# Fetching both x tiles ahead of the first K row, with dummy matmuls in between, in a linear-attention kernel

## The chip, the cores and the metric

The kernel runs on one core of a Trainium2 chip. The metric is the device time of one execution in microseconds (us), as the median of several. TensorE is called PE in the profile, VectorE DVE, ScalarE ACT, GpSimd POOL, and SyncE's DMA queue SPq. The "clock" of TensorE is the rate at which its matmuls follow one another; in these traces it has a slow and a fast value, 0.107 and 0.056 us for 128 columns.

## The reference, cut to what matters

```python
x = A_x                                             # 1 x 2048 x 1024
g = sigmoid((x * gate_w).sum(-1, keepdims=True))
a = linear_attention(x, wqkv) @ wo                  # 32 heads of 32
b = x + (gated MLP of the one row with the highest x @ w_r, put back)
return g * a + (1 - g) * b
```

Only the very start matters here: K and V are `x @ wqkv`, and this kernel feeds x to TensorE with its columns on the partitions. The sixteen x tiles have 128 rows each. Most are brought in transposed by DMA; the first two are loaded as they are and transposed on TensorE, so that work can begin early.

## The kernel before

The loads, all on SyncE's queue, 256 KB each (`load_k(c)` loads rows 128c to 128c+127 of the K weights):

```python
load_x(0, 1)
load_k(0)
load_x(1, 1)
for c in range(1, KC):          # KC = 8
    load_k(c)
# then a part of V's columns, the transposing loads, the rest of V, wq
```

TensorE's program, whose order is fixed:

```python
warm(N_WARM)                    # 6 dummy matmuls of 512 columns
...
def first_mm(t, c0, c1):        # tile t, K rows c0 to c1-1
    for c in range(c0, c1):
        for nb in range(2):
            kv_mm(first[t][nb], t, nb, c, c + 1)      # 128x512

unit_T(0)                       # 8 transposes of x tile 0, then two copies
warm(3, 128)                    # 3 dummies of 128 columns
first_mm(0, 0, 1)
wps = ps_ffn.tile([P, 16], BF, tag="f")
pe.transpose(wps[:], wrg_rows[:], ident[0:16, 0:16])
dve.tensor_copy(...)
unit_T(1)
for c in range(1, KC):
    first_mm(0, c, c + 1)
    if c < KC - 1:
        first_mm(1, c - 1, c)
es = [phi_exp(first[0][nb][:]) for nb in range(2)]
first_mm(1, 6, 8)
# ... from here on the V, K, Q and output blocks, not touched
```

I call the 32 matmuls of `first_mm` the first block: two tiles, eight K rows, two halves. In the profile's lines `warm_ps` marks the dummies, `xnat` an x tile as loaded, `pst` its transposes, `wps` the small transpose, `wkv` the K and V weights, `first` the first block and `ps` the blocks after it. `x8` means eight instructions merged into one line.

## Time and profile before

| | before |
|---|---|
| median of 3 runs (range) | 249.49 us (248.97 to 249.51) |
| span of the profiled execution | 247.7 us |
| TensorE busy | 98% of the span |
| the first block enters its dense run at, ends at | 7.17 us, 13.81 us |
| K row 1 lands at | 7.13 us |

The lines behind these numbers are in the prediction. The end of the first block is read as the start of the piece that follows it in the chain of waits (13.81, `PE ps`).

### The profile page before, as it was taken

What the parts mean: (1) busy time and instruction counts of PE and PEld (TensorE: products, weight loads), DVE (VectorE), ACT (ScalarE), POOL (GpSimd) and SP (SyncE); (2) the same over time, 40 slices, a digit from 0 to 9 for tenths busy, and PEclk for the clock granted to TensorE, in tenths of its full rate; (3) what the DMA queues carried; (4) which work ended last, traced back from release to release, by engine and by line L of the source; (5) the groups of instructions that cost most, each with busy time, mean ns of one, the idle gap of its engine ahead of it and who ended that gap; (6) DMA issues with size and microseconds to landing.
All of it is one profiled execution on the core that took longest, in us unless ns stands there. A gap on an engine that the chain in (4) does not pass through costs nothing.

```text
span 247.7 us, 4893 instructions
## 1 busy us (share of the span) xinstructions
PE 242.3 (98%) x1923; PEld 123.6 (50%) x1923; DVE 172.7 (70%) x264; ACT 127.6 (52%) x215; POOL 52.6 (21%) x100
## 2 busy tenths in 40 slices
PE   7999999999999999999999999999999999999994
PEld 3465756754554554554554555544443444444442
DVE  0043125279985879845989999996779999954342
ACT  3095434456565466544565555668887633333300
POOL 6000000300000100000013300101666689950000
PEclk9999999999999999999999999999999999999999
DMA  6999994399969992589659892000004654564122
GB/s 193 352 229 201 260 393 157 101 337 335 275 178 314 343 288 76 155 294 396 227 166 425 298 252 58 3 2 24 0 3 127 196 181 155 150 192 168 47 83 86
DMA packets 46311, 47.78 MB, mean 193 GB/s; under 512 B 16776, under 2 KB 35472, under 8 KB 46224
## 3 DMA queue, kind: packets, MB, share of 16 engines
q1 hardware_dynamic: 45648, 46.28, 61.1%
q0 software_dynamic: 608, 1.19, 1.8%
q8 instruction: 15, 0.25, 0.4%
q14 instruction: 8, 0.07, 0.1%
q10 hardware_dynamic: 32, 0.00, 0.0%
HBM read 39.33 MB, written 8.39 MB: 193 GB/s over the span
## 4 chain that ended last, share of the span: by engine, by line
PE 95%; DMA 2%; SPq 1%; DVE 0%; issue 0%; DVEq 0%
PE ps L83 88%; PE first L83 3%; PE kvacc L83 2%; DMA wkv<-in_A_wqkv_dram 2%; PE red L83 1%; PE dps L83 1%; PE pm L83 1%; SPq L83 1%; DVE ot L83 0%; PE yps L83 0%; DVEq L737 0%; PE pt L83 0%; PE hps L83 0%; PE rps L83 0%; PE xs_ps L83 0%
## 5 line engine op out<-in xcount | busy, mean ns | idle before, releaser
L83 PE MATMUL ps<-wkv,xT 128*128 128x352 bf16 (+2 forms) x608 | 106.5, 334 | 0.0
L83 PEld LDWEIGHTS <-xT 128*128 128x128 bf16 x640 | 62.2, 98 | 49.3 <-issue 0.6
L83 ACT ACTIVATE u<-ps 128x512 f32<-128x512 f32 x60 | 35.9, 598 | 46.4 <-PE ps L83 46.2
L83 PE MATMUL ps<-xT,wq 128*128 128x512 bf16 x256 | 58.4, 379 | 0.0
L83 PE MATMUL ps<-m_sb,pq_all 128*128 128x512 bf16 (+2 forms) x264 | 55.6, 373 | 0.0
L83 ACT ACTIVATE e<-u 128x512 f32<-128x512 f32 x64 | 40.3, 630 | 2.0
L83 PEld LDWEIGHTS <-pq_all 128*128 128x128 bf16 x264 | 25.4, 98 | 30.2 <-issue 0.7
L640 POOL TENSOR_TENSOR pq_all<-pq_all,rb 128x512 bf16<-128x512 bf16 x32 | 36.5, 1166 | 12.1 <-DVE rb L83 11.7
L83 PEld LDWEIGHTS <-wq 128*128 128x128 bf16 x256 | 24.4, 98 | 28.4 <-issue 1.4
L83 DVE SCALAR_TENSOR_TENSOR gacc<-wt,hcol,gacc 128x1024 f32<-128x1024 bf16 x27 | 34.5, 1279 | 0.4
L83 DVE SCALAR_TENSOR_TENSOR ot<-ps,gate,xg 128x512 bf16<-128x512 f32 (+2 forms) x33 | 23.5, 723 | 14.3 <-PE ps L83 14.2
L83 DVE SCALAR_TENSOR_TENSOR gacc<-wt,xs_f,gacc 128x2048 f32<-128x2048 bf16 x14 | 32.8, 2346 | 0.2
L83 ACT ACTIVATE xg<-xt,omg 128x1024 f32<-128x1024 bf16 x16 | 18.1, 1146 | 26.9 <-DVE ot L83 25.9
L83 DVE SCALAR_TENSOR_TENSOR pq_all<-ps,e 128x512 bf16<-128x512 f32 x32 | 21.9, 686 | 11.3 <-ACT e L83 11.3
L83 DVE SCALAR_TENSOR_TENSOR pk<-ps,e 128x512 bf16<-128x512 f32 x28 | 19.1, 686 | 11.8 <-ACT e L83 11.8
L83 DVE STREAM_SHUFFLE rb<-rdp 128x512 f32<-128x512 f32 x32 | 22.5, 731 | 0.0
L83 ACT CAST vt<-ps 128x352 bf16<-128x352 f32 x32 | 14.4, 453 | 11.5 <-PE ps L83 11.1
L214 POOL MEMSET vt<- 128x22 bf16 x16 | 3.8, 441 | 75.8 <-PE kvacc L83 75.3
L83 ACT CAST vc<-ps 128x320 bf16<-128x320 f32 x16 | 6.5, 428 | 7.3 <-PE ps L83 7.3
L83 DVE COPY rg<-ps 128x2 f32<-128x2 f32 x16 | 2.5, 159 | 10.2 <-ACT vc L83 10.1
L355 POOL DMA_DIRECT2D xs<-in_A_x_dram x1 | 0.7, 711 | 39.8 <-DVE sig L83 39.8
L83 DVE SCALAR_TENSOR_TENSOR pk<-first,e 128x512 bf16<-128x512 f32 x4 | 2.8, 692 | 8.2 <-ACT e L83 8.2
(100 smaller groups left out, 94.0 us busy)
## 6 DMA issues: line engine op xcount, KB each, us to landing
wt<-in_B_w_down_dram SPq DMA_DIRECT2D x14, 512.0 KB, 5.5
wt<-in_B_w_gate_dram SPq DMA_DIRECT2D x8, 512.0 KB, 7.4
wt<-in_B_w_up_dram SPq DMA_DIRECT2D x8, 512.0 KB, 6.4
xt<-xp SPq DMA_DIRECT2D x16, 256.0 KB, 2.6
out_dram<-ot SPq DMA_DIRECT2D x15, 256.0 KB, 2.0
wt<-in_B_w_gate_dram SPq DMA_DIRECT2D x8, 384.0 KB, 7.8
wt<-in_B_w_up_dram SPq DMA_DIRECT2D x8, 384.0 KB, 7.1
wkv<-in_A_wqkv_dram SPq DMA_DIRECT2D x8, 256.0 KB, 5.1
```

The source lines that it names most:

```text
L83: inst = fn(*a, **k)
L214: nc.gpsimd.memset(vt_t[t][:, :, 32:33], 1.0)
L355: nc.gpsimd.dma_start(out=xs8[:], in_=x2d[bass.ds(idx_val, 1), :].rearrange("o (c p) -> (o c) p", p=P))
L640: nc.gpsimd.tensor_tensor(sl, sl, rb[:], op=ALU.mult)
```

## The change

The intent: have the transposes of x tile 1 done before the K rows come, and keep TensorE busy meanwhile, so that its clock rises early. The whole diff:

```diff
     load_x(0, 1)
-    load_k(0)
     load_x(1, 1)
-    for c in range(1, KC):
+    for c in range(KC):
         load_k(c)
@@
     unit_T(0)
-    warm(3, 128)
-    first_mm(0, 0, 1)
-    wps = ps_ffn.tile([P, 16], BF, tag="f")
+    wps = ps_t.tile([P, 16], BF, tag="t")
     pe.transpose(wps[:], wrg_rows[:], ident[0:16, 0:16])
     dve.tensor_copy(wkv[:, :, 2 * D : 2 * D + 2], wps[:].rearrange("p (w c) -> p c w", w=2))
+    warm(2, 128)
     unit_T(1)
+    warm(4, 128)
+    first_mm(0, 0, 1)
     for c in range(1, KC):
```

## The prediction

> **What bounds the kernel now.** I read four views in this order: the page's first two parts, the chain of the work that ended last, the timeline of the first microseconds, and the single transfers that this timeline waits for.
>
> The page says which engine fills the span.
>
> ```profile
> span 247.7 us, 4893 instructions
> PE 242.3 (98%) x1923; PEld 123.6 (50%) x1923; DVE 172.7 (70%) x264; ACT 127.6 (52%) x215; POOL 52.6 (21%) x100
> PE   7999999999999999999999999999999999999994
> ```
>
> TensorE (PE) is busy 98% of the time, and only the first and the last of the 40 slices have holes. The change touches nothing but the start, so the question is what ends the start. The chain of waits, cut to its head, answers it (start, length, what).
>
> ```profile
> 1.90 0.45 SPq L83
> 2.35 0.04 issue
> 2.40 4.73 DMA wkv<-in_A_wqkv_dram
> 7.13 0.04 issue
> 7.17 6.64 PE first L83 x30
> 13.81 22.67 PE ps L83 x152
> ```
>
> From 7.17 us on, the chain is nearly all TensorE to 243.6 us. Before that it is one transfer: the weight row issued at 2.40 us and landed at 2.40 + 4.73 = 7.13 us. That is the fourth load on SyncE's queue, K row 1 (the order is x tile 0, K row 0, x tile 1, K row 1). So nothing that TensorE does before 7.13 us sets the end, unless it is still doing it then. The timeline of TensorE shows what it does.
>
> ```profile
> 1.02 2.72 PE L83 MATMUL warm_ps<-const-bfloat16-1.0 128*128 128x512 bf16 x6 [1.02 <-PEq L726]
> 3.88 1.03 PE L83 MATMUL pst<-ident,xnat 128*128 128x128 bf16 x8
> 4.71 0.53 PE L83 MATMUL warm_ps<-const-bfloat16-1.0 128*128 128x128 bf16 x3
> 5.03 0.85 PE L83 MATMUL first<-wkv,xT 128*128 128x512 bf16 x2
> 5.81 0.18 PE L83 MATMUL wps<-ident,wrg_rows 16*128 16x16 bf16 x1
> 6.36 0.62 PE L83 MATMUL pst<-ident,xnat 128*128 128x128 bf16 x8 [0.37 <-DMA xnat<-in_A_x_dram]
> 7.17 6.64 PE L83 MATMUL first<-wkv,xT 128*128 128x512 bf16 x30 [0.19 <-DMA wkv<-in_A_wqkv_dram]
> ```
>
> The reader is to see two holes ended by a transfer: 0.37 us for x tile 1 before its eight transposes, and 0.19 us for K row 1 before the dense run. The transposes of tile 1 end at 6.98 us, only 0.19 us ahead of the start that K row 1 allows. After it, 30 matmuls take 6.64 us, or 0.22 us each, without a wait.
>
> The times from issue to landing, asked one transfer at a time, are 2.8 us for x tile 0 (landed near 3.8), 3.0 for K row 0 (1.45 + 3.0 = 4.45), 4.4 for x tile 1 (1.90 + 4.4 = 6.3), 4.7 for K row 1 and 5.0 for K row 2 (2.87 + 5.0 = 7.87). The third load is the odd one, 1.85 us behind the second, where the others come about 0.7 us apart.
>
> **What the Trainium skill says.** "DMA: Bandwidth & Descriptors", section "Why a DMA increments its semaphore by 16 and not by 1", says that a transfer is spread over up to 16 DMA engines that finish independently, and that only the full count means that all has landed. So a load is as late as its slowest engine. This trace agrees at least with landings that don't come evenly: the third load took 4.4 us against 3.0 for the second, at equal size (256 KB).
>
> The same page, section "Queues, rings and completion order", says that on each DMA engine the descriptors are consumed in ring order. Then the landing of the fourth load depends on the bytes ahead of it, not on which tensor they belong to: this is what my prediction rests on. In the trace the loads land in the order of issue; no run here yet shows what a swap does.
>
> "TensorE: Matmul & The Clock Gate", section "Part 1: The HAM clock gate (the "warmup" mystery)", says that TensorE runs at half its clock until it has been busy for a window of about 3.4 us that runs freely. The trace agrees in the durations: the two matmuls on K row 0 start 0.42 us apart (5.03 and 5.45), those after 7.17 us come 0.22 us apart, so the clock rose somewhere between 5.4 and 7.2 us. This is what the dummy matmuls are for.
>
> **The change, part by part.**
>
> The load order becomes x tile 0, x tile 1, K row 0, K row 1, and so on. All four are 256 KB on the same queue, issued at the same four moments. If a place in the queue keeps its landing time, x tile 1 lands at 4.45 us in place of 6.3, K row 0 at 6.3 in place of 4.45, and K row 1 stays at 7.13. Later loads wait for older transfers to return their semaphores, but these are counted by place too (I compared the two built programs), so the queue's later schedule stays.
>
> On TensorE the six first dummies stay. Working with the slow rate, 0.107 us for 128 columns (the three dummies from 4.71 to 5.03 us):
> - The transposes of tile 0 run as before, to 4.71 us.
> - The small transpose of the router's and gate's rows comes next, ahead of K row 0 in place of after it: some 0.08 us, to 4.8. Its two little loads are on the other queue, issued before 1.9 us. I take them as landed, as the trace shows no wait for them at 5.81 us but can't show when they came.
> - Two dummies, 2 x 0.107 = 0.21, to 5.0 us. x tile 1 has been there since 4.45, so no wait is left: the 0.37 us hole is gone.
> - Eight transposes of tile 1, 8 x 0.107 = 0.86, to about 5.86 us. Their copies on VectorE (0.42 us) and ScalarE (0.59 us) end by about 6.5. The buffers that they need were freed by copies that end near 5.1 us.
> - Four dummies: 0.22 us if the clock is up by then, 0.43 if not: to 6.1 or 6.3 us.
> - K row 0 lands at 6.3 us: two matmuls, 2 x 0.22 = 0.43, to about 6.75.
> - Then TensorE is idle to 7.17, because the next in its program order is the pair of tile 0 on K row 1. The pair of tile 1 on K row 0, which could fill this hole, stands after that pair in the program.
>
> Removed: a 0.37 us wait. Added: three dummies net, 3 x 0.107 = 0.32 us, and a new hole of about 0.4 us. All of it lies ahead of 7.13 us, beside the transfer that sets it. The number of real matmuls left at 7.17 us is 30 in both kernels: 30 x 0.22 = 6.64 us, to 13.81. So the sum on the path is 0.0 us. What it buys is room: TensorE is ready for K row 1 at 6.75 in place of 6.98 us, 0.42 in place of 0.19 us ahead. In an execution where x tile 1 comes late, or K row 1 early, this is worth up to 0.2 us; I allow 0.1 us for it.
>
> After 13.81 us the order of instructions on every engine is the same in both built programs.
>
> **The rivals.**
>
> First rival, the intent: with both x tiles transposed early, the K stream starts sooner. It would need K row 1 to land sooner, since the program order holds all else behind it. For it speaks the odd 1.85 us step before the third load: if the slow share belongs to reading x tile 1 and not to the place in the queue, K rows 0 and 1 could come up to about 0.4 us earlier. Against it, K row 1 came only 0.8 us after x tile 1, so the engines had moved on. It would give about 248.9 us.
>
> Second rival, the clock: if the holes of TensorE after 6.1 us, or an unlucky place of the free window, keep it slow beyond 7.17 us, each matmul there costs 0.21 us more. A whole window more would be 3.4 us at half speed, a loss of 1.7 us, to 251.2; a part of one is likelier, 0.2 to 0.5 us. Against it: the row of small transposes and dummies leaves TensorE busy almost without a hole from 3.88 to about 6.2 us, more than before, where it stood idle from 5.99 to 6.36.
>
> Third rival, the dummies themselves on the path: with everything before 7.17 us at the slow clock, the four dummies end at 6.3 us and the first two matmuls take 0.85, to 7.2: 0.03 us late. Even then it costs nothing that can be seen.
>
> Fourth, K row 0 in the third place is late by more than here: it must land after 7.13 - 0.43 = 6.7 us to cost anything; it would then cost its lateness, some tenths.
>
> **Range and chances.** The start is 7.17 of 249.5 us, and no rival but the whole lost window moves it by over half a microsecond. From the 249.49 us of before I take 0.1 us for the added room: 249.4. The three runs of before spread from 248.97 to 249.51, so a median may wander by 0.3 us by itself; with the first rival's 0.5 us below and the second's 0.5 us above, 8 in 10 lie between 248.7 and 250.0. Two per cent is 5 us, most of the whole start: faster 0.01, same 0.98, slower 0.01.
>
> **What would show it.** Right: the chain still begins with the load of K row 1 and enters the dense matmuls at 7.1 to 7.3 us, with 30 of them left; x tile 1's hole is gone, its transposes start near 5.0 us; K row 0 lands near 6.3; a hole of about 0.4 us stands before K row 1; the time from the dense start to the end is the same to 0.2 us. Wrong: K row 1 lands before 6.9 us (first rival); matmuls 0.42 us apart after 7.17 us (second); the chain runs through the dummies or through K row 0 (third and fourth).

## The result, and the profile after

The changed kernel took 248.98 us (median of 4, 248.76 to 249.07), the kernel before in the same rounds 249.23 us (248.83 to 249.51). The ratio is 0.999, with an interval from 0.9971 to 1.0008: the same. Ratios here are the mean time of one kernel's fast runs over the mean of the other's in the same rounds, so not quite the ratio of the medians. The ratios of the experiments below come out of the record to 0.0001 when the first execution of each kernel, the profiled one, is left out; so 252.67 us, the longest run of all, is in no ratio.

The chain of waits at the start of the changed kernel (start, length, what):

```profile
1.02 2.72 PE warm_ps L83 x6
3.74 1.01 PE pst L83 x8
4.75 0.12 PE wps L83
4.88 0.33 PE warm_ps L83 x2
5.20 0.85 PE pst L83 x8
6.06 0.43 PE warm_ps L83 x4
6.48 4.37 PE first L83 x20
10.85 0.05 issue
10.90 2.54 PE first L83 x11
13.44 2.60 PE ps L83 x19
```

There is no transfer in it any more. The first block ends at 13.44 us, 0.37 us earlier than before, and the span is 0.3 us shorter. The timeline of TensorE for the same stretch (start, length, engine, line, operation, output<-inputs, shapes, count; in brackets the idle time before, and what ended it):

```profile
4.81 0.39 PE L83 MATMUL warm_ps<-const-bfloat16-1.0 128*128 128x128 bf16 x2
5.00 1.06 PE L83 MATMUL pst<-ident,xnat 128*128 128x128 bf16 x8
5.85 0.63 PE L83 MATMUL warm_ps<-const-bfloat16-1.0 128*128 128x128 bf16 x4
6.28 7.16 PE L83 MATMUL first<-wkv,xT 128*128 128x512 bf16 x31
```

None of these lines ends in a wait in brackets. The transposes of tile 1 start at 5.00 us and the dummies behind them at 5.85, within 0.01 us of the prediction. That is partly luck: the transposes of tile 0 began 0.16 us earlier than before (3.72 against 3.88), and 0.14 us stood empty before the small transpose. But the first block runs without a stop from 6.28 us (31 of its 32 matmuls are in the record), where I had put a hole before K row 1. Asked one by one, x tile 1 landed at 1.44 + 2.9 = 4.3 us, K row 0 at 1.89 + 3.8 = 5.7 and K row 1 at 2.4 + 4.3 = 6.7 us, not 7.13. TensorE was the last to be ready, though only just: K row 1 landed 0.09 us before the first matmul that uses it, at 6.80. Had the order of the loads brought K row 1 forward, or was this one execution lucky?

### The profile page after: what moved, and what is told of

It is laid out like the page before. It is cut to its first block, busy times and chain, and to the rows that moved or that the text cites. A ratio compares the mean times of both kernels' runs of the same rounds, so it can differ in the third digit from the quotient of the medians.

```text
span 247.4 us, 4873 instructions
## 1 busy us (share of the span) xinstructions
PE 241.0 (97%) x1901; PEld 124.3 (50%) x1926; DVE 172.7 (70%) x264; ACT 127.7 (52%) x215; POOL 52.7 (21%) x100
## 4 chain that ended last, share of the span: by engine, by line
PE 97%; issue 1%; DVE 0%; DVEq 0%
PE ps L83 88%; PE first L83 3%; PE kvacc L83 2%; PE warm_ps L83 1%; PE red L83 1%; PE pst L83 1%; PE dps L83 1%; PE pm L83 1%; DVE ot L83 0%; PE yps L83 0%; DVEq L737 0%; PE pt L83 0%; PE hps L83 0%; PE rps L83 0%; PE wps L83 0%
## 5 line engine op out<-in xcount | busy, mean ns | idle before, releaser
L83 PE MATMUL ps<-xT,wq 128*128 128x512 bf16 x246 | 57.6, 379 | 0.7 <-issue 0.3
L83 DVE SCALAR_TENSOR_TENSOR ot<-ps,gate,xg 128x512 bf16<-128x512 f32 (+2 forms) x33 | 24.0, 738 | 14.3 <-PE ps L83 14.2
```

Of the source, the lines that this page charges most:

```text
L83: inst = fn(*a, **k)
```

## The experiments

All outputs are right. Twelve runs of ten kernels were made, on three chips, each beside the kernel before on the same chip. Theory A says that the order of the loads moved K row 1; theory B, that its landing wanders in either order. Later theory C says that the clock of TensorE, and so the holes in its early work, decides; D, that it does not.

**The two kernels again, unchanged.**

> The kernel before, unchanged, to see how far its start moves between executions. Theory A (the order of the loads brought K row 1 in earlier: 6.71 us in the profile of the changed kernel against 7.13 here): x tile 1 again lands after 6.0 us, K row 1 at 7.0 to 7.3 us, dense matmuls enter at 7.1 to 7.3. Theory B (K row 1's landing wanders between executions whatever the order, and the changed kernel's profile was a lucky one): K row 1 lands anywhere from 6.6 to 7.3 us. Time 249.2 within 0.4 us.

Measured: 249.09 us against 248.94 in the same rounds. In this execution of the very same kernel x tile 1 landed at 1.91 + 3.3 = 5.2 us and K row 1 at 2.39 + 3.5 = 5.9, earlier than either theory had allowed (B gave 6.6 to 7.3). The gate became K row 2. Chain and TensorE's timeline, a few lines of each:

```profile
2.87 4.31 DMA wkv<-in_A_wqkv_dram
7.18 0.04 issue
7.22 3.83 PE first L83 x17
...
12.99 3.14 PE ps L83 x23
```

```profile
5.34 0.62 PE L83 MATMUL pst<-ident,xnat 128*128 128x128 bf16 x8
5.96 1.02 PE L83 MATMUL first<-wkv,xT 128*128 128x512 bf16 x4
7.22 5.77 PE L83 MATMUL first<-wkv,xT 128*128 128x512 bf16 x25 [0.24 <-DMA wkv<-in_A_wqkv_dram]
```

The first block of the kernel before ended at 12.99 us here, earlier than that of the changed kernel in any of its profiles.

> The changed kernel, unchanged. Theory A: K row 1 lands at 6.6 to 6.9 us again and the chain holds no transfer before the dense matmuls. Theory B: in this execution it may land after 7.0 us and gate again. Time 249.0 within 0.4 us; ratio to before 0.998 to 1.000 in both.

Measured: 249.01 us, ratio 1.0016 (0.9996 to 1.0035). K row 1 gates again, as my prediction had it, though at 6.51 us. So neither theory was met to the letter: A had no transfer in the chain, B had K row 1 after 7.0 us if it gated.

```profile
2.39 4.12 DMA wkv<-in_A_wqkv_dram
6.52 0.04 issue
6.56 4.04 PE first L83 x18
```

Theory B's core, that the landing wanders in either order, holds as far as the profiles go: with the order of before (three profiles, one of them of `pe_only` below), K row 1 landed at 7.13, 5.9 and 6.4 us; with the new order (eleven profiles, those of all kernels below included), at 6.3 to 7.2. The two groups overlap, and one kernel alone spans 1.2 us. No sign is left that the new order brings K row 1 forward.

**One half of the change at a time.** `loads_only` is the kernel before with the loads of the changed one:

```diff
     load_x(0, 1)
-    load_k(0)
     load_x(1, 1)
-    for c in range(1, KC):
+    for c in range(KC):
```

> The kernel before with the loads alone swapped (x tile 1 ahead of K row 0), TensorE's order as before. Theory A: K row 0 lands near 5.75 us, K row 1 near 6.7; TensorE waits for K row 0 in third place, then does two matmuls and the eight transposes of tile 1 after it: dense matmuls enter at 6.9 to 7.3 us with 30 left, no better than before: ratio 1.000 within 0.001. Theory B: the same, with K row 1 anywhere from 6.6 to 7.3 us.

Both expectations missed: ratio 1.0066 (1.0029 to 1.0103), median 251.07 us, and runs from 249.35 to 252.67. The profiled execution (252.67 us) shows why, in TensorE's timeline:

```profile
4.45 0.52 PE L83 MATMUL warm_ps<-const-bfloat16-1.0 128*128 128x128 bf16 x3
6.31 1.01 PE L83 MATMUL first<-wkv,xT 128*128 128x512 bf16 x2 [1.33 <-DMA wkv<-in_A_wqkv_dram]
7.37 1.03 PE L83 MATMUL pst<-ident,xnat 128*128 128x128 bf16 x8
8.20 8.77 PE L83 MATMUL first<-wkv,xT 128*128 128x512 bf16 x29
```

TensorE stood still for 1.33 us waiting for K row 0, now the third load. After that its work is slow: the transposes of tile 1 take 1.03 us, against 0.62 in the profile of before, and the rest of the block takes 8.77 us, against 6.64. How slow is read from the same stretch of both kernels, the kernel before first (stretch, its length, then PE's busy time and its number of matmuls, PEld's, and so on; PEclk is the printed clock):

```profile
8.40:12.50 4.10, 4.10 (x21) 1.86 (x19) 0.00 (x0) 0.00 (x0) 0.00 (x0) 1.00 1.20 353
```

```profile
8.40:12.50 4.10, 4.10 (x12) 1.39 (x10) 0.04 (x1) 0.59 (x1) 0.00 (x0) 1.00 1.20 346
```

In 4.1 us TensorE did 12 matmuls in place of 21, though busy all the time in both. The printed clock is 1.00 in both: that column does not show the slow clock at the start, the number and the durations of the matmuls do (611 to 634 ns recorded for one in this stretch, 379 after it). The block ends at 16.97 us, 3.2 us late, which is the lengthening of the execution to 0.1 us: about 1.0 us of it is the later start (8.20 against 7.17), 2.1 us the slower matmuls (8.77 against 6.64).

`pe_only` is the other half: TensorE's order and dummies of the changed kernel, the loads in the order of before.

```diff
     load_x(0, 1)
+    load_k(0)
     load_x(1, 1)
-    for c in range(KC):
+    for c in range(1, KC):
```

> TensorE's order of the changed kernel with the loads in the order of before. Transposes of tile 1 wait for x tile 1 in third place. If that lands near 6.3 us as in the profile of before: eight transposes to 6.8 to 7.0, four dummies to 7.2, then all 32 matmuls from 7.2 us at 0.22 each: end of them near 14.2 us, 0.4 us after before, ratio 1.001 to 1.002. If the third place lands near 5.75 us as in the changed kernel's profile (theory B): dense matmuls at 6.7 us, end near 13.7, ratio 0.999 to 1.001.

Measured: ratio 1.0029 (1.0005 to 1.0052), 249.5 us. In its profile TensorE waited 0.99 us for x tile 1, which landed at 5.72 us; the block ended at 13.53. The profile is that of theory B, the ratio lies a little above what I had given it. So each half alone costs time, 0.3 to 0.7%; together no cost is seen. Why the second half costs is not shown: its profile is of one of its two short executions (249.11 us; the long ones took 249.88 and 249.94).

**Is it the hole before K row 0?** The swap of the loads was run again, and with more dummies in the hole.

> The kernel with only the loads swapped once more, for the spread: its runs so far went from 249.35 to 252.67 us, and in its profile the matmuls stayed at the slow clock to about 12.5 us. Theory C (the hole of 1.3 us before K row 0 makes TensorE miss a busy window, so the clock stays slow one or two windows longer, depending on where the free window lies): runs spread from 249 to 252.7 us again, ratio 1.004 to 1.010. Theory D (that execution was an accident of the chip): 249.0 within 0.4 us, ratio near 1.000.

Measured: ratio 1.0056 (1.0026 to 1.0087); runs of 249.36, 249.48, 249.80, 250.79, 251.32 and 251.35 us. The profile fell on the shortest, and there the clock was already up when the hole came: its transposes of tile 0 took 0.70 us against 1.03 in the first profile, and the two matmuls after a hole of 1.36 us were recorded at 376 ns each:

```profile
3.76 0.70 PE L83 MATMUL pst<-ident,xnat 128*128 128x128 bf16 x8
5.99 0.59 PE L83 MATMUL first<-wkv,xT 128*128 128x512 bf16 x2 [1.36 <-DMA wkv<-in_A_wqkv_dram]
```

So in this execution a hole of 1.36 us did not bring a risen clock down; in the first profile a hole of 1.33 us came before the rise, and the rise came only at 12.5 us.

```diff
     unit_T(0)
-    warm(3, 128)
+    warm(15, 128)
     first_mm(0, 0, 1)
```

> The same with twelve more dummies of 128 columns in that hole (15 in place of 3, 1.6 us at the slow clock). No load and no real matmul differs. Theory C: the clock rises by 4.2 to 7.6 us, the first block of 32 matmuls ends at 13.3 to 14.3 us, no run above 250, ratio 0.999 to 1.002: dummy work makes the kernel faster by 1 to 2 us against the same without. Theory D: no better than loads_again or slower by the dummies.

Measured: ratio 1.0014 (0.9994 to 1.0034), 249.53 us, runs from 249.29 to 249.87. Timeline:

```profile
4.49 1.81 PE L83 MATMUL warm_ps<-const-bfloat16-1.0 128*128 128x128 bf16 x15
6.08 1.01 PE L83 MATMUL first<-wkv,xT 128*128 128x512 bf16 x2
7.59 6.68 PE L83 MATMUL first<-wkv,xT 128*128 128x512 bf16 x29
```

No load and no real matmul differs from `loads_again`; twelve matmuls whose result nobody reads were added, and the mean of the six fell by 0.8 us (250.35 to 249.56; by 1.05 us without the profiled executions, as the ratios take it). The 1 to 2 us that I had expected were about met. The rest of the block now takes 6.68 us, at full rate, and the long executions are gone. The intervals of the two ratios still overlap; what carries the argument is the count: 6 of the 10 runs of the swap alone lie above 250.7 us, none of the 12 with more dummies (these six and the six of `loads_half` below) above 249.9. This shows that the empty stretch makes the long executions, as theory C says. That the late clock is what lengthens them is seen in one profile, the first of `loads_only`; the profiles of `loads_again` and `loads_half` fell on the shortest run of each.

> The swap of the loads alone with six more dummies (nine in place of three): half of the hole before K row 0 is filled, 0.3 to 0.7 us stay. Theory C with a tolerance of some tenths of a microsecond (the kernel before keeps its clock with holes of 0.37 and 0.19 us): between loads_again (ratio 1.0056, runs to 251.35) and loads_fill (1.0014, to 249.87): ratio 1.001 to 1.004, at most two runs above 250. Without tolerance: as loads_again.

Measured (`warm(9, 128)` in that place): ratio 1.0013 (0.9995 to 1.0030), no run above 249.73 us. In its profile K row 0 came early, at 5.08 us, and only 0.19 us of hole was left, so the tolerance was not tested as planned. What its profile does show is an early rise, with transposes of tile 0 that are fast from 3.85 us on, 2.8 us after TensorE's first dummy:

```profile
3.77 0.63 PE L83 MATMUL pst<-ident,xnat 128*128 128x128 bf16 x8
```

**The dummies of the change.** `no_dummies` is the changed kernel without them:

```diff
-    warm(2, 128)
     unit_T(1)
-    warm(4, 128)
     first_mm(0, 0, 1)
```

> The changed kernel without the six dummies (two and four) around the transposes of tile 1. Theory C: TensorE waits 0.3 to 0.8 us for K row 0 and more for K row 1, so in some executions a window is missed and the clock rises late: ratio 1.001 to 1.005 with a run or two above 250. Theory D: the six dummies are only time on the path: ratio 0.998 to 1.000.

Measured: five runs from 249.13 to 249.25 us and one of 250.85; ratio 1.0015 (0.9987 to 1.0043). The profile fell on an ordinary run, with holes of 0.48 us before K row 0 and 0.24 before K row 1 and a clock already up; its chain starts with K row 2. The one long run fits a missed clock, but nothing shows what it was, and the kernel before had one of 250.24 in the same rounds. Inconclusive.

`double` has four times as many dummies ahead of the transposes of tile 1, 0.64 us more at the slow clock:

```diff
-    warm(2, 128)
+    warm(8, 128)
     unit_T(1)
```

> The changed kernel with eight dummies in place of two ahead of the transposes of tile 1: 6 x 0.107 = 0.64 us more on TensorE at the slow clock, 0.34 at the fast one. If TensorE is the bound from the transposes on (as in the first profile of the changed kernel): the first block ends 0.3 to 0.6 us later, ratio to before 1.001 to 1.003. If the landing of K rows 0 and 1 gates (as in the second): the slack of 0.3 to 0.6 us takes most of it, ratio 0.999 to 1.001.

Measured: ratio 1.0010 (0.9995 to 1.0025), which settles nothing. The profile shows the slack at work:

```profile
4.79 0.76 PE L83 MATMUL warm_ps<-const-bfloat16-1.0 128*128 128x128 bf16 x8
6.06 0.59 PE L83 MATMUL first<-wkv,xT 128*128 128x512 bf16 x2
7.24 6.63 PE L83 MATMUL first<-wkv,xT 128*128 128x512 bf16 x29 [0.58 <-DMA wkv<-in_A_wqkv_dram]
```

K row 0 had landed at 1.91 + 3.5 = 5.4 us, and TensorE, held by dummies and transposes, came to its two matmuls 0.7 us later; yet K row 1, late at 7.20 us in this execution, set the start.

`no_first` is the changed kernel with `N_WARM = 0`, so TensorE stands idle to 3.76 us (the 3.4 us in the expectation is the window for which the prediction cites the Trainium skill):

> The changed kernel without the six dummies of 512 columns at the start, so that TensorE stands idle to about 3.7 us. Theory C (the clock needs a busy window of some 3.4 us): the clock rises only 3.4 to 6.8 us after 3.7, at 7.1 to 10.5 us; TensorE loses half of the slow time after 6.3 us: 0.4 to 2.1 us, ratio 1.002 to 1.008, and the runs spread by over 1 us. If a window counts as busy with less than all of it: smaller, 1.001 to 1.004.

Measured: ratio 1.0039 (1.0015 to 1.0062); four runs from 249.36 to 249.69 and two at 250.74 and 250.76. In its profile the block, entered at 6.32 us as in the changed kernel, takes 7.69 us in place of 7.16. The first two matmuls start 0.42 us apart and the rate rises at about 7.4 us, within the 7.1 to 10.5 expected. Theory C again: what is lost is rate, not start.

**A version to beat both.** `fill_row0` lets work that needs only K row 0 go ahead of work that needs K row 1:

```diff
-        first_mm(0, c, c + 1)
         if c < KC - 1:
             first_mm(1, c - 1, c)
+        first_mm(0, c, c + 1)
```

> The changed kernel with the pair of tile 1 on a K row ahead of the pair of tile 0 on the next row, so that the hole before K row 1 is filled by work that needs only K row 0. If K row 1 gates (my prediction): dense work starts at K row 0, the 32 matmuls end up to 0.4 us earlier, ratio 0.998 to 0.9995. If TensorE itself is the bound from the transposes on, as in the first profile of the changed kernel: no change, ratio 0.999 to 1.001.

Measured: 249.00 us, ratio 0.9993 (0.9971 to 1.0014): not told apart from the kernel before. Its profile shows how little is left to win. The end of its chain at the start:

```profile
6.09 7.16 DMA wkv<-in_A_wqkv_dram
13.25 0.05 issue
13.29 2.77 PE ps L83 x19
```

The dense run was entered at 6.12 us and the block was done about 13.2 us, but the next block had to wait for the V columns, which landed at 13.25. In the profile of before the same load landed at 6.33 + 6.9 = 13.2 us, only 0.6 us ahead of the end of the block.

**The last comparison.**

> The changed kernel once more, in more rounds, for the size of its difference. Ratio 0.998 to 1.001; the two earlier comparisons gave 0.999 and 1.0016. Where in the queue the slow landings fall should differ again from its other two profiles: x tile 1 at 4.2 to 4.7 us, K row 0 at 5.2 to 6.3, K row 1 at 5.9 to 7.1.

Measured: ratio 1.0003 (0.9987 to 1.0020), and landings within the ranges given: 4.4, 5.3 and 6.9 us. Over all rounds on several chips, the changed kernel's 14 runs have a median of 248.99 us, the kernel before's 37 (with `b_again`) one of 249.00.

The profiles side by side:

| profile | third load at | K row 1 at | block ends | span | span less block end |
|---|---|---|---|---|---|
| before | 6.3 | 7.13 | 13.81 | 247.7 | 233.9 |
| b_again | 5.2 | 5.9 | 12.99 | 247.0 | 234.0 |
| after | 5.7 | 6.7 | 13.44 | 247.4 | 234.0 |
| a_again | 5.3 | 6.5 | 13.19 | 247.2 | 234.0 |
| a_five | 5.3 | 6.9 | 13.56 | 247.5 | 233.9 |
| loads_only | 6.3 | 7.0 | 16.97 | 251.0 | 234.0 |
| pe_only | 5.7 | 6.4 | 13.53 | 247.5 | 234.0 |

The last column is constant to 0.1 us. All that differs between these executions, by order, luck or clock, lies in the first block.

## Why the prediction was right or wrong

- **The time** was right: 249.4 predicted, 248.98 measured, within the range. It proves little for the mechanism, which by its own signs was wrong in the first profile: the chain held no load of K row 1, which landed at 6.71 us (under the 6.9 named as a sign of being wrong), and the dense run began at 6.28 us with 32 matmuls left, not at 7.1 to 7.3 with 30. The time came out right because the start is so small a part. The statement that two per cent is out of reach of the start was right too.
- **TensorE's steps up to 6.3 us** were right: transposes of tile 1 at 5.00 us, dummies at 5.85, the wait for x tile 1 gone; the dummies' start by errors that cancel, as said above. The clock was read too loosely: the lines shown place its rise before 6.36 us (the transposes of tile 1 took 0.62 us, those of tile 0 1.03), not only before 7.2.
- **"If a place in the queue keeps its landing time" failed.** The third place was at 6.3 us in the profile of before and at 5.1 to 6.3 in the other thirteen; K row 1, said to stay at 7.13 us, came between 5.9 and 7.2. I took one execution's landings for a property of the queue. The page that I cited gives the order in which each engine takes up descriptors; that a place then has a landing time was my own step. The odd 1.85 us step that I had noted before the third load wanders too: 0.9 us in `b_again`, 2.0 in `loads_only`.
- **The hole of 0.4 us before K row 1** was therefore not in the first profile, whose chain runs through transposes, dummies and matmuls, as my third rival had it; in `a_again` K row 1 gated. The gate changes with the execution: K row 1, K row 2 or TensorE. Between these two profiles of the changed kernel it is the clock that differs: in the first, matmuls came at the slow rate up to 6.3 us, so the dummies and transposes were on the path; in `a_again` the rate had risen by 4.4 us, TensorE was done early and waited.
- **"The sum on the path is 0.0 us" held, for a wider reason.** It is 0.0 on average, not because one transfer always gates. The block ended at 13.81 and 12.99 us in the two profiles of before, at 13.44, 13.19 and 13.56 in the three of the changed kernel: 13.40 us on average in both. That the wandering of landings and clock hides any smaller effect is my reading of these five.
- **The first rival** (K row 1 sooner, 248.9 us) came nearest in time in the first comparison, yet its reason fell: K row 1 came as early in the old order (5.9 and 6.4 us).
- **The second rival**, the clock, was not seen in any of the changed kernel's three profiles; that an empty stretch there would be costly was right, and larger than "0.2 to 0.5 us" and than the 1.7 us of a whole window: 2.1 us of rate in `loads_only`, 3.2 with the hole. The new order of TensorE's work is what makes the new load order harmless. Which part of it does, the dummies or the early transposes, is not told apart: `no_dummies` was inconclusive. I had priced the dummies as 0.32 us added beside a transfer; that the new order pays for the swap, the prediction did not say.

What stays open: how much idle time the warm-up tolerates (the last section has an estimate), why TensorE's half of the change costs time alone, and what makes a load land late.

## What to carry to other kernels

Before you build on the landing time of one transfer, look at it in a second execution of the same kernel; a reorder worth less than that spread could not be told from none here. If a reorder of loads opens a hole in TensorE's first microseconds, fill it with independent matmuls, even dummies, and judge by the spread of many runs, since one run may be lucky with its clock. When a start-up block looks improvable, check first when the next block's own load lands: here it left 0.6 us in the profile of before.

## What the Trainium skill lacked or had wrong

- "TensorE: Matmul & The Clock Gate", section "Part 1: The HAM clock gate (the "warmup" mystery)", has the warm-up depend on a window that runs freely. The runs agree: one unchanged kernel (`loads_only` and `loads_again`) took 249.35 to 252.67 us, and with the same six dummies from 1.02 us on, and no hole or a short one before the rise, the fast rate began between 3.8 us (`loads_half`) and 6.9 us (`loads_fill`). It doesn't say how much idle time a window that counts as busy may hold. Here a hole of 1.33 us kept the clock slow to about 12.5 us in one execution, while a hole of 1.36 us after the rise left it up. An estimate, from the starts of the matmuls in all fourteen profiles and the window of about 3.4 us that this section states: windows that the rise followed hold at most 0.8 to 0.9 us of idle time (`loads_half` has the most), windows that it did not follow at least 0.8 to 0.9 us (`loads_only`, then `loads_fill`), so the limit would lie near 0.9 us. The transposes count as busy in this, as they must in `no_first`: the rate rose at about 7.4 us there, although 17 of the 26 instructions up to then were transposes.
- "DMA: Bandwidth & Descriptors", section "Why a DMA increments its semaphore by 16 and not by 1", says that the engines finish independently, but I found no figure there for how far the landing of a load wanders from one execution to the next: the third of equal loads of 256 KB took 3.2 to 4.4 us from issue to landing in the fourteen profiles. That the engines' independence is the cause is not shown.
